# Gate bias seeded by ScalarE in PSUM for 15 of 36 blocks, three last adds on VectorE, and a new order, in a windowed-attention and highway kernel

## The chip, the cores and the metric

The kernel runs on one core of a Trainium2 chip. The metric is the device time of one execution in microseconds (us); a smaller number is better. Before the change the median of 3 runs is 156.6 us (155.8 to 159.38).

The engines are called PE or TensorE (matrix products, writing to PSUM), DVE or VectorE, ACT or ScalarE, POOL or GpSimd (which also issues all loads) and SP or SyncE (which issues the stores). PSUM has eight banks of 512 fp32 columns.

## The reference

Sliding-window attention with a linear distance bias, then a highway layer (cut to what matters):

```python
# q, k, v: (8, 8, 576, 64) float32: batch, heads, positions, head size
scores = q @ k^T / sqrt(64) - slope[head] * |i - j|      # only where 0 <= i - j < 128
attn = softmax(scores)
x = (attn @ v), heads side by side                       # (4608, 512)
H = relu(x @ w_h)
T = sigmoid(x @ w_t + b_t)                               # b_t: (512,), the gate bias
out = T * H + (1 - T) * x                                # (4608, 512) float32
```

## The kernel before

The attention is cut into 32 units (batch b of 8, group of four heads s of 2, half of the key tiles g of 2), and the highway layer into 36 blocks of 128 rows of x (four or five per batch; a block numbered 4 gathers the first 64 rows of two batches).

A unit takes these steps, each named by a letter. T (`tr`, L183): VectorE transposes loaded bf16 data of q or k. s (`scores`, L190): TensorE writes scores to banks 0 to 3. e (`soft`, L234): ScalarE takes the exponential to SBUF. m (`mask`, L241): VectorE multiplies with a table that holds the distance bias and the window; for the units in `MASK_PE` this step is left out, and four TensorE matmuls (L197) put the bias into PSUM ahead of the scores. p (`pv`, L246): TensorE multiplies with v and a column of ones, into two of banks 4 to 7. n (`norm`, L281): VectorE takes reciprocals and scales into x.

A block takes these. x and c (L311, L317): TensorE transposes x into PSUM and ScalarE copies it to SBUF. h (`mm_h`, L321): four matmuls with w_h. u (`relu_sub`, L333): VectorE computes relu(h) - x straight from PSUM (L339), or, for blocks in `RELU_ACT`, ScalarE first does the relu (r, L331) and VectorE subtracts from SBUF (L336). z (`mm_z`, L343): four matmuls with w_t, and a fifth (L349) that adds the bias as a product of `ones0`, whose first row is one, with `bT`, whose first row is the bias. a (`tanh`, L353): ScalarE takes the tanh of half the sum. t (L357, ScalarE) or, for blocks in `GATE_DVE`, k (L361, VectorE): the scaling 0.5 + 0.5 tanh, which gives T. g (`gate`, L366): VectorE multiplies T with relu(h) - x. o (`add_x`, L370): GpSimd adds x. d (`store`, L377): SyncE stores the rows.

L (`load`, L119) issues one of 60 loads from GpSimd's queue, in the order of the list `LOADS`; GpSimd runs loads and adds in one order. The loads cast fp32 in memory to bf16 in SBUF.

The work order is not left to a scheduler: the string `ORDER`, a plan made beforehand, is read letter by letter, and a digit behind s, p, x, h and z is the (first) PSUM bank. Each letter takes the next entry of its list, so each engine runs its instructions in the order in which they stand in the string. Banks 0 to 3 belong to the scores; p, x, h and z share banks 4 to 7. An instruction waits for whatever wrote its inputs and for whatever last used its outputs.

Of the kernel before, what the change touches and what calls it, by code (L numbers as in the profile page):

```python
# [9 lines left out]
P = 128  # L10
# [1 line left out]
NLD, NTR, NPB = 20, 12, 8  # L12


RELU_ACT = (1, 5, 6, 7, 8, 12, 14, 15, 16, 17, 23)
GATE_DVE = (0, 10, 16, 22, 24, 26, 28, 29)

LOADS = (0, 1, 3, 4, 2, 6, 5, 12, 16, 9, 14, 10, 13, 11, 17, 8, 15, 18, 20, 7, 21, 22, 27, 26, 19, 31, 29, 25, 30, 23, 24, 32, 33, 28, 34, 35, 39, 38, 40, 36, 41, 43, 37, 44, 46, 45, 53, 42, 47, 48, 58, 49, 52, 50, 56, 57, 51, 54, 59, 55)

MASK_PE = (6, 12)  # L20


ORDER = (
    "SLLSSLLLTLLTLs0LTLeLTLSms0LLp4LeLTLms0LLnp6eLLns0Lmx4ex5TLp6cms0cnep4Lz6nLmx7az4cTLSp6Tz"
    "5ns0ah6eh4ux7ks0mcrgap6Toth4enLdz5TLh6auLtux5Ls0ucx4eTx7z5gcTs0oah6cgLedmp4h7nous0rLdmh4"
    "tLez5Tp6grus0aonz4eTLdx5p6mcLs0th5nLaemp6z4ntgrx6Tx7aox5s0cgcducToh4ttp6mLdez5LnTp6rs0ag"
    "h4ueunoz5uLds0maLx4tp6Tez5gncos0az4TeLdx5mp6cLagLs0nth5eLTp6Lz4ontux6Lads0kmch5egh4mp6ru"
    "os0tnx4ez5Lduggh6mcx4z7gcToah4auodx5Trp6tods0cnh4eLdmz5LurgLx6maz7LtuLp4Tas0tLnh7coeTp4d"
    "h6gnros0rTx7p4cduex6z7nux4mz5acgcx7mz6atkTp4oats0nLdh6egp4Lguocs0Th6eLdnoz7uLx4dz5mcaLgh"
    "4amtx5p6Tocs0uh5edgz4noutp6amds0h4negh5uotx6Tz4cLdmp6as0rnz4egTox5p6aks0cLdnx4ez5umh6cTa"  # L30
    "h4ux5us0cz6geToh7mtds0akp4geuoh6nx7kdp4gcms0z7enouz4admp6amts0nx4h5cgp6uox4nz5cdgp6akotx"
    "4nh5egdz6uocx5h7cgdkgx4h5mcaz4uoup6oadtz5tdgz4ganoth5aodtx4h6ucgdx7z4uoch5gadotz4ugdh5ao"
    "tudgod"
)


def lists():

    units = [(b, s, g) for b in range(NB) for g in range(NG) for s in range(NS)]
    blocks = []  # L40
    for b in range(NB):
        blocks += [(b, 0), (b, 1)] + ([(b, 4)] if b % 2 else []) + [(b, 2), (b, 3)]
    trs = [(b, s, w) for b in range(NB) for s in range(NS) for w in range(2)]
    loads = []
    for b in range(NB):
        n = 1 if b < 2 else 2
        vs = [("v", b, n, m) for m in range(5)] if b < 2 or b % 2 == 0 else []
        ts = [("t", b, s, w) for s in range(NS) for w in range(2)]
        if b == 0:
            loads += ts[:2] + vs[:1] + ts[2:] + vs[1:3] + [("w", 0), ("w", 1), ("w", 2)] + vs[3:]  # L50
        else:
            loads += ts[:2] + vs[:3] + ts[2:] + vs[3:]
    by = dict(L=[loads[i] for i in LOADS], T=trs, S=list(range(5)))
    by.update({k: units for k in "sepn"})
    by["m"] = [u for i, u in enumerate(units) if i not in MASK_PE]
    by["pe_mask"] = [units[i] for i in MASK_PE]
    by.update({k: blocks for k in "xchuzagod"})
    by["r"] = [blocks[i] for i in RELU_ACT]
    by["k"] = [blocks[i] for i in GATE_DVE]
    by["t"] = [bk for i, bk in enumerate(blocks) if i not in GATE_DVE]  # L60
    return by
# [3 lines left out]
def kernel(  # L65
# [19 lines left out]
    ALU = mybir.AluOpType  # L85
# [4 lines left out]
    NC = DM // P  # L90
# [4 lines left out]
    by = lists()  # L95
# [23 lines left out]
    def load(kind, *at):  # L119
        if kind == "t":  # L120
            b, s, w = at
            nc.gpsimd.dma_start(
                out=LD[(4 * b + 2 * s + w) % NLD][:],
                in_=(q, k)[w][b, 4 * s : 4 * s + 4].rearrange("h (p t) d -> (h p) (t d)", t=NT))
        elif kind == "v":
            b, n, m = at
            rows, h = min(P, S - m * P), b % 2 * H
            nc.gpsimd.dma_start(  # L128
                out=VA[b // 2][0:rows, h : h + n * H, m, 0:D],
                in_=v[b : b + n, :, m * P : m * P + rows].rearrange("b h p d -> p (b h) d"))  # L130
        elif at[0] < 2:
            nc.gpsimd.dma_start(
                out=(wH, wT)[at[0]][:],
                in_=(moe_w_h, moe_w_t)[at[0]].rearrange("(c p) n -> p c n", p=P))
        else:
            nc.gpsimd.dma_start(out=bT[0:1, :], in_=moe_b_t.rearrange("(o n) -> o n", o=1))

    def setup(part):
        if part == 0:
            for i in range(NB // 2):  # L140
                nc.vector.memset(VA[i][:, :, :, D:E], 1.0)
            nc.vector.memset(PS[D:P, 0:4, 0:D], 0.0)
            nc.vector.memset(bT[:], 0.0)
            nc.vector.memset(ones0[:], 0.0)
            nc.vector.memset(ones0[0:1, :], 1.0)
            nc.vector.memset(ident[:], 1.0)
        elif part == 1:
            rel = cp.tile([P, 256], I32, name="rel_i")
            far = cp.tile([P, 256], F32, name="far")
            nc.gpsimd.iota(rel[:, 0:192], pattern=[[1, 192]], base=64, channel_multiplier=-1)  # L150
            nc.gpsimd.iota(rel[0:D, P:192], pattern=[[1, D]], base=0, channel_multiplier=-1)
            nc.gpsimd.iota(rel[:, 192:256], pattern=[[1, D]], base=0, channel_multiplier=-1)
            nc.gpsimd.affine_select(
                out=ident[:], in_=ident[:], compare_op=ALU.is_equal, fill=0.0,
                base=0, pattern=[[1, P]], channel_multiplier=-1)
            nc.vector.tensor_copy(out=REL[:], in_=rel[:])
            nc.vector.tensor_scalar(out=far[:], in0=REL[:], scalar1=-63.5, scalar2=None,
                                    op0=ALU.add)
            nc.vector.tensor_tensor(out=far[:], in0=far[:], in1=far[:], op=ALU.mult)
            nc.vector.tensor_scalar(out=far[:], in0=far[:], scalar1=4096.0, scalar2=1.0e6,  # L160
                                    op0=ALU.is_gt, op1=ALU.mult)
            nc.vector.tensor_tensor(out=REL[:], in0=REL[:], in1=far[:], op=ALU.add)
        elif part == 4:
            for h in range(H):
                nc.scalar.activation(out=SI[:, h, :], in_=ident[:], func=ACTF.Copy,
                                     scale=-slopes[h] / scale)
            nc.scalar.copy(out=RB[:, 0:D], in_=REL[:, 192:256])
# [175 lines left out]
    def mm_z(b, i, bank):  # L343
# [4 lines left out]
                             start=c == 0, stop=False)  # L348
        nc.tensor.matmul(out=pz, lhsT=ones0[:], rhs=bT[:], start=False, stop=True)  # L349

    def tanh(b, i):
        tt = TT[b, i] = ft.tile([P, DM], F16, name="tt")
        nc.scalar.activation(out=tt[:], in_=PZ.pop((b, i)), func=ACTF.Tanh, scale=0.5)  # L353
# [14 lines left out]
    def add_x(b, i):  # L368
        ot = OT[b, i] = ft.tile([P, DM], F32, name="ot")
        nc.gpsimd.tensor_tensor(out=like(ot[:], i), in0=like(UU.pop((b, i))[:], i),  # L370
                                in1=xview(b, i), op=ALU.add)

    def store(b, i):
        ot = OT.pop((b, i))
        if i < 4:
            row = b * S + D + i * P
            nc.sync.dma_start(out=out[row : row + P, :], in_=ot[:])  # L377
            return
        for r in range(2):
            row = (b - 1 + r) * S  # L380
            nc.sync.dma_start(out=out[row : row + D, :], in_=ot[r * D : (r + 1) * D, :])

    do = dict(L=load, T=tr, S=setup, s=scores, e=soft, m=mask, p=pv, n=norm, x=x_tr, c=x_copy,
              h=mm_h, u=relu_sub, z=mm_z, a=tanh, t=to_gate, k=to_gate_v, r=relu, g=gate, o=add_x, d=store)
    at = dict.fromkeys(by, 0)
    steps = iter("".join(ORDER))
    with tc.manual_schedule():
        for step in steps:
            what = by[step][at[step]]
            what = what if isinstance(what, tuple) else (what,)  # L390
            at[step] += 1
            if step in "spxhz":
                bank = int(next(steps))
                what += (bank,)
            do[step](*what)
# [30 lines left out]
```

## Time and profile before

| what | value |
|---|---|
| median of 3 runs | 156.6 us |
| the profiled execution | 156.49 us |
| its span, first to last instruction | 153.8 us |
| mean granted TensorE clock | 0.991 |
| L370 GpSimd add, 36 of them | 46.5 us, mean 1293 ns |
| L349 bias matmul on TensorE, 36 of them | 13.7 us, mean 379 ns |
| L353 tanh on ScalarE, 36 of them | 21.6 us, mean 601 ns |
| L357 gate scaling on ScalarE, 28 of them | 17.4 us, mean 629 ns |
| L361 gate scaling on VectorE, 8 of them | 3.4 us, mean 422 ns |
| L366 gate multiplication on VectorE, 36 of them | 17.9 us, mean 502 ns |
| L243 mask on VectorE, 15 of 1792 and 15 of 1536 columns | 17.2 us, mean 1145 ns; 14.4 us, mean 958 ns |

A line of the page's list of groups gives busy time, mean duration of one instruction, and the idle time of the engine ahead of it with what ended that. The rows of matmuls overlap: a 512-column matmul has a row of some 380 ns, while the next one starts 216 ns behind it. The stretches of the span (in us from its start) are cut where the chain of work that ended last changes its engine.

### The profile page before, as it was taken

To read this page: it belongs to the slowest core of one execution; us is meant where nothing else is said; L and a number is where in the kernel's file an instruction comes from. 1 tells how busy PE (TensorE), PEld (TensorE's weight loads), DVE (VectorE), ACT (ScalarE), POOL (GpSimd) and SP (SyncE) were. 2 spreads that over 40 slices of the span, in tenths; PEclk is the share of its full clock that TensorE was granted. 3 is DMA by queue.
4 is the path that set the end of the run, shared out by engine and by line. 5 is a ranking of instruction groups with operands and counts; after the bars stand their busy time and mean duration, and the time that the engine had idled before them with its cause. 6 is when DMAs were issued, how large, how long until landed. Compare 5 with 4: busy or idle time off the path is not lost.

```text
span 153.8 us, 5756 instructions
## 1 busy us (share of the span) xinstructions
PE 127.1 (83%) x2495; PEld 79.8 (52%) x2524; DVE 136.0 (88%) x220; ACT 115.4 (75%) x170; POOL 91.8 (60%) x104
## 2 busy tenths in 40 slices
PE   0027698999997998999959799799999999999950
PEld 0026584565655664665535566546575557644420
DVE  4865898699999999999999999999999999897650
ACT  3658476998998988898867969578887965667740
POOL 6986844157956467595889235797341370577562
PEclk9999999999999999999999999999999999999996
DMA  2999999999999989999999991899977212243353
GB/s 37 192 146 174 194 196 199 212 199 175 146 234 240 198 205 125 193 157 183 238 285 168 192 234 49 103 213 201 193 142 110 72 72 68 75 154 119 136 156 119
DMA packets 48233, 25.01 MB, mean 163 GB/s; under 512 B 38480, under 2 KB 39504, under 8 KB 48208
## 3 DMA queue, kind: packets, MB, share of 16 engines
q0 software_dynamic: 42960, 15.21, 91.8%
q1 hardware_dynamic: 5248, 9.44, 17.6%
q8 instruction: 19, 0.31, 0.8%
q14 instruction: 6, 0.05, 0.1%
HBM read 30.41 MB, written 9.44 MB: 259 GB/s over the span
## 4 chain that ended last, share of the span: by engine, by line
DVE 34%; PE 33%; DMA 15%; issue 9%; POOL 3%; ACT 1%; POOLq 1%; DVEq 0%; ACTq 0%
DVE tr L183 10%; PE ps L347 10%; PE ps L324 9%; DMA wT<-in_moe_w_t_dram 6%; DVE x L289 5%; DMA va<-in_v_dram 5%; DMA ld<-in_q_dram 5%; DVE p L243 5%; DVE uu L366 4%; DVE uu L339 3%; PE ps L212 3%; PE ps L275 3%; DVE uu L336 3%; PE ps L349 2%; PE ps L254 2%
## 5 line engine op out<-in xcount | busy, mean ns | idle before, releaser
L370 POOL TENSOR_TENSOR ot<-uu,x 128x512 f32<-128x512 bf16 x36 | 46.5, 1293 | 50.6 <-DVE uu L366 28.5
L238 ACT ACTIVATE p<-ps 128x1792 bf16<-128x1792 f32 (+1 forms) x32 | 49.9, 1559 | 12.3 <-PE ps L224 12.1
L183 DVE STREAM_TRANSPOSE tr<-ld 128x576 uint32<-128x576 uint32 x32 | 39.9, 1248 | 3.5 <-DMA ld<-in_q_dram 2.7
L347 PE MATMUL ps<-wT,xt 128*128 128x512 bf16 x132 | 36.3, 383 | 1.0 <-DMA wT<-in_moe_w_t_dram 0.3
L324 PE MATMUL ps<-wH,xt 128*128 128x512 bf16 x127 | 35.1, 381 | 1.1 <-issue 0.2
L243 DVE TENSOR_TENSOR p<-p,mt 128x1792 bf16<-128x1792 bf16 (+1 forms) x30 | 31.5, 1051 | 0.0
L353 ACT ACTIVATE tt<-ps 128x512 f16<-128x512 f32 x36 | 21.6, 601 | 8.7 <-PE ps L349 6.6
L212 PE MATMUL ps<-tr,tr 32*64 32x192 bf16 (+1 forms) x1024 | 18.2, 258 | 11.4 <-DVE tr L183 11.1
L128 POOL DMA_DIRECT2D va<-in_v_dram x25 | 25.4, 1019 | 1.8 <-DMA va<-in_v_dram 1.2
L319 ACT COPY xt<-ps 128x512 bf16<-128x512 bf16 x36 | 20.7, 587 | 6.4 <-PE ps L314 6.4
L289 DVE TENSOR_TENSOR x<-ps,rd 128x512 bf16<-128x512 f32 (+1 forms) x32 | 24.3, 758 | 1.2
L339 DVE SCALAR_TENSOR_TENSOR uu<-ps,x 128x512 bf16<-128x512 f32 x25 | 16.8, 682 | 3.9 <-PE ps L324 3.9
L212 PEld LDWEIGHTS <-tr 32*64 32x64 bf16 x1024 | 11.6, 111 | 16.4 <-DVE tr L183 11.6
L254 PE MATMUL ps<-va,p 128*128 128x65 bf16 x256 | 14.4, 200 | 6.8 <-DVE x L289 2.4
L347 PEld LDWEIGHTS <-xt 128*128 128x128 bf16 x144 | 12.7, 98 | 12.4 <-issue 0.8
L254 PEld LDWEIGHTS <-p 128*128 128x128 bf16 x256 | 12.1, 101 | 13.1 <-issue 7.4
L324 PEld LDWEIGHTS <-xt 128*128 128x128 bf16 x144 | 12.4, 98 | 12.3
L366 DVE TENSOR_TENSOR uu<-uu,tt 128x512 bf16<-128x512 bf16 x36 | 17.9, 502 | 0.8 <-ACT tt L357 0.3
L357 ACT ACTIVATE tt<-tt 128x512 f16<-128x512 f16 x28 | 17.4, 629 | 0.1
L275 PE MATMUL ps<-va,p 64*64 64x65 bf16 x448 | 14.9, 202 | 0.0
L314 PE MATMUL ps<-ident,x 128*128 128x128 bf16 x144 | 13.9, 224 | 0.7 <-DVE uu L339 0.7
L314 PEld LDWEIGHTS <-x 128*128 128x128 bf16 x144 | 10.2, 99 | 6.9 <-issue 1.6
(43 smaller groups left out, 107.3 us busy)
## 6 DMA issues: line engine op xcount, KB each, us to landing
out_dram<-ot SPq DMA_DIRECT2D x32, 256.0 KB, 3.8
ld<-in_q_dram POOLq DMA_DIRECT2D x16, 288.0 KB, 7.1
ld<-in_k_dram POOLq DMA_DIRECT2D x16, 288.0 KB, 8.0
va<-in_v_dram POOLq DMA_DIRECT2D x12, 256.0 KB, 7.4
va<-in_v_dram POOLq DMA_DIRECT2D x11, 128.0 KB, 6.8
out_dram<-ot SPq DMA_DIRECT2D x8, 128.0 KB, 2.4
wT<-in_moe_w_t_dram POOLq DMA_DIRECT2D x1, 512.0 KB, 8.5
wH<-in_moe_w_h_dram POOLq DMA_DIRECT2D x1, 512.0 KB, 10.8
```

The lines of the kernel that those rows point to most:

```text
L128: nc.gpsimd.dma_start(out=VA[b // 2][0:rows, h : h + n * H, m, 0:D], in_=v[b : b + n, :, m * P : m * P + rows].rearrange("b h p d -> p (b ...
L183: nc.vector.transpose(out=TR[i % NTR][:].rearrange("p s e -> p (s e)").bitcast(U32).rearrange("p (s t) -> p t s", t=NT), in_=LD[i % NLD][: ...
L212: nc.tensor.matmul(out=PS[r * D : r * D + D, bank + a, c0:c1], lhsT=KT[rows, lo + r * D : lo + r * D + D, e], rhs=QT[rows, q0 : q0 + c1 - ...
L238: nc.scalar.activation(out=PB[i][:, :, 0:w], in_=PS[:, bank : bank + 4, 0:w], func=ACTF.Exp, scale=scale)
L243: nc.vector.tensor_tensor(out=p[:, :, 0:w], in0=p[:, :, 0:w], in1=MT[s][:, :, 448 - w : 448] if g else MT[s][:], op=ALU.mult)
L254: nc.tensor.matmul(out=PS[:, bank + o, a * E : a * E + E], lhsT=p[:, a, col : col + P], rhs=VA[b // 2][:, b % 2 * H + 4 * s + a, i, :], st ...
L289: nc.vector.tensor_tensor(out=X[b, g][:, s, :, 0:n, :], in0=av[:, :, 0:n, 0:D], in1=rd[:, :, 0:n, :].to_broadcast([P, 2, n, D]), op=ALU.mult)
L314: nc.tensor.transpose(out=XP[b, i][:, c * P : (c + 1) * P], in_=xchunk(b, i, c), identity=ident[:])
L324: nc.tensor.matmul(out=pa, lhsT=XT[b, i][:, c, :], rhs=wH[:, c, :], start=c == 0, stop=c == NC - 1)
L347: nc.tensor.matmul(out=pz, lhsT=xt[:, c, :], rhs=wT[:, c, :], start=c == 0, stop=False)
L366: nc.vector.tensor_tensor(out=uu, in0=uu, in1=TT.pop((b, i))[:], op=ALU.mult)
L370: nc.gpsimd.tensor_tensor(out=like(ot[:], i), in0=like(UU.pop((b, i))[:], i), in1=xview(b, i), op=ALU.add)
```

## The change

For 15 blocks (`BIAS_ACT`) the step z is replaced by w and y. In w (`bias`), ScalarE copies the bias, now on all 128 partitions, into the block's PSUM bank; in y (`mm_y`), four matmuls that do not start a new sum add onto it. The fifth matmul falls away for these blocks. The bias is loaded into all 128 rows of `bT`, and the memset of `bT` is gone. The other 21 blocks keep z; there `ones0` still picks out the first row.

For the last three blocks (`ADD_DVE`), the add of x is done on VectorE (q) and not on GpSimd.

`MASK_PE` has four units in place of two, `GATE_DVE` 17 blocks in place of 8, `RELU_ACT` 12 in place of 11. `LOADS` and `ORDER` are new; they were planned with a rule that VectorE and GpSimd exclude each other in some instructions.

```diff
-RELU_ACT = (1, 5, 6, 7, 8, 12, 14, 15, 16, 17, 23)
-GATE_DVE = (0, 10, 16, 22, 24, 26, 28, 29)
+RELU_ACT = (2, 4, 7, 8, 12, 15, 16, 18, 21, 26, 30, 31)
+GATE_DVE = (0, 1, 2, 4, 5, 11, 14, 17, 21, 22, 24, 25, 26, 27, 28, 32, 33)
-LOADS = (0, 1, 3, 4, 2, 6, 5, 12, 16, 9, 14, 10, 13, 11, 17, 8, 15, 18, 20, 7, 21, ...)
+LOADS = (0, 1, 3, 4, 6, 5, 2, 12, 10, 13, 17, 11, 18, 8, 9, 7, 31, 15, 14, 16, 21, ...)
+BIAS_ACT = (1, 4, 8, 11, 12, 16, 18, 20, 23, 26, 27, 29, 32, 34, 35)
+ADD_DVE = (33, 34, 35)
-MASK_PE = (6, 12)
+MASK_PE = (7, 12, 14, 26)
...
-            nc.gpsimd.dma_start(out=bT[0:1, :], in_=moe_b_t.rearrange("(o n) -> o n", o=1))
+            nc.gpsimd.dma_start(
+                out=bT[:], in_=moe_b_t.rearrange("(o n) -> o n", o=1).to_broadcast([P, DM]))
...
-            nc.vector.memset(bT[:], 0.0)
...
+    def bias(b, i, bank):
+        PZ[b, i] = PS[:, bank, :]
+        nc.scalar.copy(out=PZ[b, i], in_=bT[:])
+
+    def mm_y(b, i):
+        for c in range(NC):
+            nc.tensor.matmul(out=PZ[b, i], lhsT=XT[b, i][:, c, :], rhs=wT[:, c, :], start=False,
+                             stop=c == NC - 1, skip_group_check=True)
...
+    def add_x_v(b, i):
+        ot = OT[b, i] = ft.tile([P, DM], F32, name="ot")
+        nc.vector.tensor_tensor(out=like(ot[:], i), in0=like(UU.pop((b, i))[:], i),
+                                in1=xview(b, i), op=ALU.add)
```

In `LOADS`, entry 8 is w_t, 9 the bias and 7 w_h; 0, 1, 3, 4 and 12, 13, 17, 18 are q and k of the first two batches, 2, 5, 6, 10, 11 the values of the first.

The end of the order, written here with the batch and block of each letter in place of the bank digits:

```
before: ... z74g70a71n711o63t71h71a74o70d63t74x72h74u71c72g71d70x73z72u74o71c73h72g74a72d71o74t72z73u72g72d74h73a73o72t73u73d72g73o73d73
after:  ... o63a71z74c72u71o70w72d63h74a74k71d70x73k74y72u74c73g71w73h72g74a72q74o71y73t72u72h73d71g72d74a73q72t73d72u73g73q73d73
```

More of the change, by code (lines that the diff above doesn't have):

```diff
@@ L12 @@
 NLD, NTR, NPB = 20, 12, 8
-RELU_ACT = (1, 5, 6, 7, 8, 12, 14, 15, 16, 17, 23)
-GATE_DVE = (0, 10, 16, 22, 24, 26, 28, 29)
-LOADS = (0, 1, 3, 4, 2, 6, 5, 12, 16, 9, 14, 10, 13, 11, 17, 8, 15, 18, 20, 7, 21, 22, 27, 26, 19, 31, 29, 25, 30, 23, 24, 32, 33, 28, 34, 35, 39, 38, 40, 36, 41, 43, 37, 44, 46, 45, 53, 42, 47, 48, 58, 49, 52, 50, 56, 57, 51, 54, 59, 55)
-MASK_PE = (6, 12)
-ORDER = (
[L24 to L33, printed above, removed]
@@ new lines @@
+RELU_ACT = (2, 4, 7, 8, 12, 15, 16, 18, 21, 26, 30, 31)
+GATE_DVE = (0, 1, 2, 4, 5, 11, 14, 17, 21, 22, 24, 25, 26, 27, 28, 32, 33)
+LOADS = (0, 1, 3, 4, 6, 5, 2, 12, 10, 13, 17, 11, 18, 8, 9, 7, 31, 15, 14, 16, 21, 27, 22, 20, 26, 23, 19, 30, 24, 25, 32, 33, 34, 29, 28, 39, 35, 38, 40, 48, 46, 43, 44, 45, 36, 37, 47, 42, 41, 51, 50, 53, 52, 49, 54, 56, 58, 57, 55, 59)
+BIAS_ACT = (1, 4, 8, 11, 12, 16, 18, 20, 23, 26, 27, 29, 32, 34, 35)
+ADD_DVE = (33, 34, 35)
+MASK_PE = (7, 12, 14, 26)
+ORDER = (
+    "SLLSSLLLTLLTLs0LTLeLLTSLms0LLp4eLTLms0nLp6eTLms0Lnp4eTLx6ms0cTx7eLz6nLcp4as0w6nLh7emh4Lk"
+    "ux5LyucSmp4h7ns0aTp4regx6nz7oTx4aLx5ds0cuLw7mLch6cTeLz4Tyaus0akgp4ekox6nh7LcdTp4rLs0uh6m"
+    "ez7gnots0uax4Lekz5dTLp6gaks0Tcox5h4cnLdez5mLh6tuamh7rtgs0grTow4p6eLudynLmx5as0cuop6eTx4h"
+    "5dgncos0tuLdp6eTLp4Lns0mx6z7cnez6ggap4Toas0w7nLdx6tyocTtp4dah6genox7uh4Lmdcx5Lw6s0gLh7cm"
+    "eyLukp4Taos0rnz6tLdegLTx7h4Lamh5ctus0oux6eh7uLdgz4Trocx5z7Tcdah5maw4p6mrs0tknyegp6guoz5n"
+    "atTLx4dp6acus0Lw5mh4enyoup6admts0h4enx5gp6Tocrs0nz5LedLgx4up6ckmLas0gw5h4noeyLgdx6uoh7cT"
+    "ax4z6LdtuocTh5aLdp6mrLs0nx4h5cgmep6z4uoutns0Ladmw5p6egx4nyocTx6h7dckaz4utgz5kagTop6as0on"
+    "dh4eTdx5p6cus0nw4h5emh6Tx7yrkcus0w6gx7agymcop4eodz7namp4das0nh6ekx7up4uckw6s0nh7kx4gygcg"
+    "oux4h5comdah4tuop6drex5nz4dkgh6cumaoz5rw4gdp6toayntdx5gx6uch7goaz5cuow4dh6akdx5kyucgw7h5"
+    "gaqoytuh4dgdaqtdugqd"
@@ L57, in lists @@
     by.update({k: blocks for k in "xchuzagod"})
+    by["w"] = by["y"] = [blocks[i] for i in BIAS_ACT]
+    by["z"] = [bk for i, bk in enumerate(blocks) if i not in BIAS_ACT]
+    by["q"] = [blocks[i] for i in ADD_DVE]
+    by["o"] = [bk for i, bk in enumerate(blocks) if i not in ADD_DVE]
     by["r"] = [blocks[i] for i in RELU_ACT]
@@ L383 @@
     do = dict(L=load, T=tr, S=setup, s=scores, e=soft, m=mask, p=pv, n=norm, x=x_tr, c=x_copy,
-              h=mm_h, u=relu_sub, z=mm_z, a=tanh, t=to_gate, k=to_gate_v, r=relu, g=gate, o=add_x, d=store)
+              h=mm_h, u=relu_sub, z=mm_z, a=tanh, t=to_gate, k=to_gate_v, r=relu, g=gate, o=add_x, d=store,
+              w=bias, y=mm_y, q=add_x_v)
     at = dict.fromkeys(by, 0)
@@ L391 @@
             at[step] += 1
-            if step in "spxhz":
+            if step in "spxhzw":
                 bank = int(next(steps))
```

## The prediction

> **What bounds the kernel now.** First the page: busy shares, then the slices, then the chain that ended last.
>
> ```profile
> PE 127.1 (83%) x2495; PEld 79.8 (52%) x2524; DVE 136.0 (88%) x220; ACT 115.4 (75%) x170; POOL 91.8 (60%) x104
> ...
> PE   0027698999997998999959799799999999999950
> ...
> DVE  4865898699999999999999999999999999897650
> ...
> DVE 34%; PE 33%; DMA 15%; issue 9%; POOL 3%; ACT 1%; POOLq 1%; DVEq 0%; ACTq 0%
> ```
>
> No engine stands out: VectorE and TensorE are both near full from about 30 us, and they share the chain. So I cut the span where the chain, in order of time, changes hands (VectorE's pieces fill it from 34 to 98 us, TensorE's from 98 to 148) and asked for busy time by stretch.
>
> ```profile
> 35.00:98.00 63.00, 56.77 (x1203) 35.66 (x1217) 61.95 (x95) 54.50 (x75) 41.26 (x43) 1.00 1.39 185
> 98.00:148.00 50.00, 48.58 (x821) 29.07 (x831) 46.25 (x80) 36.87 (x53) 27.11 (x24) 1.00 0.67 130
> 148.00:153.80 5.80, 0.20 (x1) 0.00 (x0) 1.12 (x2) 0.63 (x1) 2.01 (x2) 0.75 0.44 137
> ```
>
> Columns: PE, weight load, DVE, ACT, POOL. In the first stretch VectorE is busy 61.95 of 63 us (98%), TensorE 90%; in the second TensorE 97%, VectorE 92%. Relief of one engine helps only until the other binds: TensorE has some 6 us of slack in the first stretch.
>
> VectorE's busy time is not all work. Its timeline and GpSimd's around 75 us:
>
> ```profile
> 75.17 2.04 DVE L243 TENSOR_TENSOR p<-p,mt 128x1792 bf16<-128x1792 bf16 x1
> 77.13 1.37 DVE L366 TENSOR_TENSOR uu<-uu,tt 128x512 bf16<-128x512 bf16 x1
> ...
> 75.06 3.16 POOL L370 TENSOR_TENSOR ot<-uu,x 128x512 f32<-128x512 bf16 x2 [0.73 <-DVE uu L366]
> ```
>
> Undisturbed, this mask takes 1.08 us and this gate 0.415. Each began just after a GpSimd add had begun and finished 0.96 us late; the second add in turn ran long (2.00 against 1.15 us). PSUM-reading subtractions, norms and transposes beside such adds keep their time; masks, gates, gate scalings and SBUF subtractions do not. Over the run 12 instructions are held for 7.3 us, 7 of them for 5.1 us in the first stretch.
>
> The start and the end:
>
> ```profile
> 14.94 8.54 DMA wT<-in_moe_w_t_dram
> 23.53 0.61 PE ps L347
> ...
> 149.10 0.42 DVE L366 TENSOR_TENSOR uu<-uu,tt 128x512 bf16<-128x512 bf16 x1
> 149.66 1.15 POOL L370 TENSOR_TENSOR ot<-uu,x 128x512 f32<-128x512 bf16 x1 [0.79 <-POOL ot L370]
> ```
>
> TensorE reaches its first gate matmul and waits for the weights; at the end the last add is GpSimd's, followed by a store.
>
> **The change, part by part,** against the profiled execution: 156.49 us, of which 153.8 are the span and 2.7 lie around it (the median of the runs is 156.6).
>
> *Start.* The gate weights are the 14th load in GpSimd's queue, not the 16th, and wH the 16th, not the 20th; value loads go back. The wait above cost 0.26 us ahead of the first matmul and some 0.6 us between it and the second (23.53 to 24.36, where neighbours stand 0.215 apart): 0.9 us. Two loads fewer ahead (0.56 and 0.95 us to issue) cover it. The memset of the bias tile that goes (0.27 us) ran while VectorE still waited for its first load. The bias, now 128 rows and behind the weights instead of ahead, is wanted only after the four weight matmuls (0.86 us). Ends: 0 (attention work of that moment is no earlier) and -1.5. I take **-0.9**.
>
> *First stretch, VectorE's own work.* Gate scalings there go from 2 to 7: 5 x 0.282 = +1.4 us. Two blocks return from ScalarE's relu to the subtraction from PSUM: 2 x (0.68 - 0.41) = +0.5. One mask goes to TensorE (unit 14; unit 7 replaces 6, an equal swap): -0.95. Net **+1.0**. TensorE loses 6 bias matmuls here (6 x 0.216; another of the 15 ran at 26 us) and gains a mask (0.65); VectorE paces this stretch, so I count neither.
>
> *The holds.* The new order was planned with this exclusion. The 5.1 us can go entirely. They can also grow: instructions that can be held go from 85 (36 gates, 30 masks, 11 SBUF subtractions, 8 scalings) to 96, 13% of 5.1 = +0.7. Read off the two orders, the instructions standing within 1.2 us behind a gate, where its add would run, include 34 that can be held before (36 adds) and 36 after (33 adds). That shows no cure, but ignores how long an add waits behind loads. Nothing favours an end: I take the middle, **-2.2**, and keep +0.7 and -5.1.
>
> *Second stretch, TensorE.* Eight of the 15 bias matmuls ran after 98 us: 8 x 0.216 = -1.7; a mask (unit 26) adds 4 x 0.163 = +0.65 (row mean 326 ns less the 163 ns by which a matmul's row outlasts its spacing). **-1.1.** VectorE, close behind, loses that mask (-0.95); 4 more scalings (+1.1) and 4 fewer PSUM subtractions (-1.1) cancel. Ends: 0 (VectorE or the seeds bind) and -1.7.
>
> *Seeds.* Copying bf16 from SBUF to fp32 in PSUM is not in the trace; 512-wide ScalarE rows lie between 0.587 and 0.629 us. 15 x 0.59 = +8.9, nine scalings fewer 9 x 0.63 = -5.7, a relu +0.6: ScalarE +3.8 to 119 us. I cost it at nothing: TensorE reaches the add-on one to four steps after the seed was queued, and ScalarE idles 38 us in all. The cover is thin from 40 to 55 us, where ScalarE is busy 14.04 of 15 us. Behind each seed stand exponentials and x copies that TensorE needs. If the cover is gone everywhere: +8.9; the other end is 0.
>
> *Tail.* For the last three blocks the add follows the gate on VectorE. The gate ends at 149.52, GpSimd's add at 150.81. An fp32-writing add 512 wide lies between the gate's 0.415 and the PSUM subtraction's 0.68 us; fp32 tensor ops of 256 columns take 0.425, so I take 0.69, of which 0.08 overlaps the gate: 150.13, **-0.7**. The stores on SyncE wait for VectorE instead of GpSimd. Ends: -0.9, and 0 if the two earlier adds (1.3 us) push the last gate; they lie beside TensorE's last two groups (1.7 us).
>
> Sum: -0.9 + 1.0 - 2.2 - 1.1 - 0.7 = -3.9; 156.5 - 3.9 = **152.6 us**.
>
> **Rivals.**
>
> *Seeds in the way (slower).* Seven of the 15 seeds go to a bank last read by a relu step, six of those on VectorE, which is 98% busy in the first stretch; ScalarE, in order, waits there with an exponential behind it, and TensorE waits for both. For: the thin stretch. Against: TensorE has other steps between. If each seed holds TensorE for its 0.59 us: 152.6 + 8.9 = 161.5. It decides from 0.47 us per seed (7.1 us over 15), 159.7.
>
> *Holds stay.* The chip's order of starts differs from the planned one, so adds still catch masks. For: the count of 34 and 36. No gain at the start, and +1.0 + 0.7 - 1.1 - 0.7: 156.4, no change.
>
> *Holds vanish.* -0.9 + 1.0 - 5.1 - 1.1 - 0.7 = -6.8: 149.7. Against: TensorE would have to run the first stretch at 97%.
>
> *Loads starved.* Gate scalings on VectorE might hold up GpSimd's load issue, not only its adds. In this trace no scaling overlaps a load's issue, so no row decides it. Nine more at 0.28 us, all on the path: +2.5, 155.1. The Trainium skill says this (SBUF — State Buffer, section "SBUF: two separate sides"): a VectorE instruction that uses both port pairs locks GpSimd out, descriptor writing for its DMAs included. What the trace shows agrees as far as adds go (the 0.96 us above); for loads, by the page, the sum would be 155.1 instead of 152.6.
>
> **How the numbers follow.** Forecast 0.40 (own range 150.7 to 154.5: the holds half-way to either end are 1.45 us, start and tail 0.45), holds stay 0.25, seeds in the way 0.19, holds vanish 0.13, loads starved 0.03. About 2% is what a measurement of this kernel can tell from no change: 153.5 and 159.7. Faster: 0.31 of the forecast and 0.13 = 0.44. Same: 0.09 + 0.25 + 0.03 = 0.37. Slower: 0.19. From 149.0 to 158.0 the range takes in all but the seeds' case.
>
> **What would show it.** Right: the mean of the gates (L366 before, 502 ns) falls toward 415 and fewer VectorE rows run 0.96 us long; the seeds' rows take about 0.59 us and hardly any matmul waits for them; the first gate matmul starts before 23 us; the last VectorE add ends under 0.7 us after its gate. Wrong: TensorE or ScalarE's exponentials waiting on seeds, ScalarE waiting on VectorE's subtractions, as many long rows as before, or TensorE under 90% after 98 us.

## The result, and the profile after

The changed kernel takes 161.19 us (median of four runs, 160.24 to 161.3) against 156.45 for the kernel before on the same chip: a ratio of 1.0304, 95% interval 1.0245 to 1.0363. It is 4.7 us slower where 3.9 us faster was forecast. Medians here and below are over all executions of a kernel; ratios leave out those over 1.5% longer than its fastest. The profiled execution took 161.23 us, with a span of 159.5 (before: 156.49 and 153.8).

The page of the changed kernel: busy time of each engine, and the chain that ended last, by engine.

```profile
PE 126.9 (80%) x2488; PEld 79.7 (50%) x2517; DVE 143.6 (90%) x229; ACT 119.7 (75%) x177; POOL 87.6 (55%) x101
...
DVE 49%; PE 18%; DMA 15%; issue 10%; POOL 3%; ACT 2%; DVEq 0%; POOLq 0%
```

VectorE is 7.6 us busier than before, and its share of the chain rose from 34 to 49%; TensorE's fell from 33 to 18%. The same stretches as before (columns: PE, weight load, DVE, ACT, POOL, granted clock) say where:

```profile
35.00:98.00 63.00, 57.34 (x1237) 35.88 (x1250) 60.97 (x97) 54.65 (x74) 39.63 (x42) 1.00 1.39 179
98.00:148.00 50.00, 44.00 (x785) 26.71 (x781) 48.29 (x78) 37.60 (x54) 25.83 (x24) 1.00 0.63 124
148.00:159.50 11.50, 5.34 (x28) 2.37 (x26) 8.25 (x14) 4.72 (x9) 2.46 (x3) 0.91 0.40 138
```

Up to 98 us TensorE is level with before (57.34 us busy against 56.77). Between 98 and 148 us it falls from 48.58 to 44.00 us, 88% where before it had 97%, while VectorE rises to 97%. The work that TensorE lost there is done after 148 us (5.34 us against 0.20).

VectorE is full but does less, because it is held behind GpSimd far more often. Undisturbed durations are as before (mask 1.08 or 0.95 us, gate 0.415, SBUF subtraction 0.415, scaling 0.282); the new add on VectorE takes 0.69. What each row has above them, added up over the rows that are over by 60 ns or more:

| stretch | before | after |
|---|---|---|
| to 98 us | 7 held, 5.1 us | 5 held, 3.8 us |
| 98 to 148 us | 5 held, 2.2 us | 11 held, 8.3 us |
| from 148 us | none | 2 held, 1.5 us |
| sum | 12 held, 7.3 us | 18 held, 13.7 us |

The sum grew by 6.4 us, the span by 5.7. All 12 rows before are held behind adds. Of the 18 after, 16 are, for 12.1 us; the other two are scalings held for 1.6 us behind GpSimd's issue of value loads (last section). Which instruction is held can be read in two places. First the changed kernel at 128 us, then the kernel before at 124 us, each from its timeline (start and duration in us; x2 is two instructions in a row):

```profile
127.42 0.74 DVE L382 TENSOR_TENSOR uu<-uu,tt 128x512 bf16<-128x512 bf16 x2
...
127.96 3.17 POOL L386 TENSOR_TENSOR ot<-uu,x 128x512 f32<-128x512 bf16 x2 [6.35 <-DVE uu L382]
...
128.07 2.05 DVE L250 TENSOR_TENSOR p<-p,mt 128x1792 bf16<-128x1792 bf16 x1
```

```profile
124.16 0.42 DVE L366 TENSOR_TENSOR uu<-uu,tt 128x512 bf16<-128x512 bf16 x1
...
124.50 1.09 DVE L243 TENSOR_TENSOR p<-p,mt 128x1792 bf16<-128x1792 bf16 x1
...
124.71 1.88 POOL L370 TENSOR_TENSOR ot<-uu,x 128x512 f32<-128x512 bf16 x1 [0.82 <-DVE uu L366]
```

In the second place the mask stands directly behind a gate. It starts 0.21 us before that gate's add, keeps its 1.09 us, and the add takes 1.88 us instead of 1.15. In the first place there are two gates and then the mask: the first gate's add starts while the second gate runs, 0.11 us before the mask, and the mask takes 2.05 us. So whichever starts first keeps its time, and the other waits it out. An add starts 0.13 us behind the end of its gate, and the next VectorE instruction, if it waits for nothing, some 0.08 us before that end: the first instruction behind a gate wins and the second can lose. In both traces no instruction of these kinds that began 0.16 to 0.23 us ahead of an add (11 before, 12 after) is more than 12 ns over its time. The changed order has more places where a gate with an add on GpSimd is followed by one instruction under 0.5 us and then by one that can be held: 8, before 3.

The other steps of the prediction in the trace: the chain of the start, the seeds, and the end of VectorE's timeline.

```profile
5.54 7.23 DMA va<-in_v_dram
12.77 0.28 issue
13.05 10.47 DMA wT<-in_moe_w_t_dram
...
23.57 0.58 PE ps L354
24.15 0.22 issue
24.37 1.06 PE ps L354 x2
```

```profile
L360 ACT CAST ps<-bT x15: 589/597/632, 26.5 to 150.4; 128x512 f32<-128x512 bf16 x15
...
  DVE uu L346: 1.6, 2
who waited for it (us, times):
```

```profile
155.41 0.43 DVE L382 TENSOR_TENSOR uu<-uu,tt 128x512 bf16<-128x512 bf16 x1
155.87 0.69 DVE L391 TENSOR_TENSOR ot<-uu,x 128x512 f32<-128x512 bf16 x1
```

The weights' load was issued 1.89 us earlier and took 10.47 us instead of 8.54, so the first gate matmul starts where it did (23.57, before 23.53). The seeds take 597 ns at the median, and no wait is put down to them: the list in the last line is empty. ScalarE itself waited 1.6 us, twice, to write them. The last add on VectorE ends 0.72 us behind its gate, where GpSimd's ended 1.29 behind it.

### The profile page after: what moved, and what is told of

Its sections match the earlier page's. It is cut to its first block, busy times and chain, and to the rows that moved or that the text cites. A ratio compares the mean times of both kernels' runs of the same rounds, so it can differ in the third digit from the quotient of the medians.

```text
span 159.5 us, 5747 instructions
## 1 busy us (share of the span) xinstructions
PE 126.9 (80%) x2488; PEld 79.7 (50%) x2517; DVE 143.6 (90%) x229; ACT 119.7 (75%) x177; POOL 87.6 (55%) x101
## 4 chain that ended last, share of the span: by engine, by line
DVE 49%; PE 18%; DMA 15%; issue 10%; POOL 3%; ACT 2%; DVEq 0%; POOLq 0%
DVE tr L190 10%; DVE p L250 10%; DMA va<-in_v_dram 8%; DVE uu L382 7%; DVE x L296 7%; DMA wT<-in_moe_w_t_dram 7%; DVE uu L346 6%; PE ps L331 6%; DVE uu L343 4%; DVE tt L377 2%; PE ps L354 2%; DVE rd L295 2%; PE ps L282 2%; PE ps L219 2%; PE ps L261 2%
## 5 line engine op out<-in xcount | busy, mean ns | idle before, releaser
L386 POOL TENSOR_TENSOR ot<-uu,x 128x512 f32<-128x512 bf16 x33 | 42.3, 1286 | 53.2 <-DVE uu L382 28.3
L245 ACT ACTIVATE p<-ps 128x1792 bf16<-128x1792 f32 (+1 forms) x32 | 49.9, 1559 | 11.2 <-PE ps L231 10.9
L219 PE MATMUL ps<-tr,tr 32*64 32x192 bf16 (+1 forms) x1024 | 18.7, 262 | 12.2 <-DVE tr L190 11.3
L219 PEld LDWEIGHTS <-tr 32*64 32x64 bf16 x1024 | 11.9, 112 | 17.1 <-DVE tr L190 12.3
L331 PEld LDWEIGHTS <-xt 128*128 128x128 bf16 x144 | 12.6, 98 | 12.8 <-issue 1.0
L382 DVE TENSOR_TENSOR uu<-uu,tt 128x512 bf16<-128x512 bf16 x36 | 17.1, 492 | 0.4
L321 PE MATMUL ps<-ident,x 128*128 128x128 bf16 x144 | 14.5, 225 | 3.2 <-DVE x L296 3.1
L346 DVE SCALAR_TENSOR_TENSOR uu<-ps,x 128x512 bf16<-128x512 f32 x24 | 16.2, 680 | 0.1
L373 ACT ACTIVATE tt<-tt 128x512 f16<-128x512 f16 x19 | 12.1, 635 | 0.2
```

The costliest lines, as they stand in the source:

```text
L219: nc.tensor.matmul(out=PS[r * D : r * D + D, bank + a, c0:c1], lhsT=KT[rows, lo + r * D : lo + r * D + D, e], rhs=QT[rows, q0 : q0 + c1 - ...
L245: nc.scalar.activation(out=PB[i][:, :, 0:w], in_=PS[:, bank : bank + 4, 0:w], func=ACTF.Exp, scale=scale)
L321: nc.tensor.transpose(out=XP[b, i][:, c * P : (c + 1) * P], in_=xchunk(b, i, c), identity=ident[:])
L331: nc.tensor.matmul(out=pa, lhsT=XT[b, i][:, c, :], rhs=wH[:, c, :], start=c == 0, stop=c == NC - 1)
L346: nc.vector.scalar_tensor_tensor(out=like(uu[:], i), in0=like(PA.pop((b, i)), i), scalar=0.0, in1=xview(b, i), op0=ALU.max, op1=ALU.subtract)
L382: nc.vector.tensor_tensor(out=uu, in0=uu, in1=TT.pop((b, i))[:], op=ALU.mult)
```

## The experiments

Theory A: the 4.7 us are VectorE being held behind GpSimd's adds. Rivals: the seeds (B), the gate scalings moved to VectorE (C), the new list of loads (D). Each ratio is to the kernel before, measured beside it. The holds are those of the one profiled execution. Where a kernel says "before" or "after" it starts from that one.

| kernel | us, median | ratio, 95% interval | VectorE held |
|---|---|---|---|
| after | 161.19 | 1.030 (1.025 to 1.036) | 18, 13.7 us |
| before, add without its reads | 151.16 | 0.965 (0.954 to 0.975) | 3, 0.9 us |
| after, add without its reads | 153.35 | 0.979 (0.969 to 0.988) | 3, 1.7 us |
| after, no seeds | 161.05 | 1.030 (1.023 to 1.037) | 20, 14.0 us |
| after, 12 scalings on ScalarE | 160.57 | 1.027 (1.019 to 1.036) | 16, 12.3 us |
| after, add in two halves | 156.83 | 1.008 (1.003 to 1.013) | 23, 9.6 us |
| before, add in two halves | 152.96 | 0.981 (0.974 to 0.988) | 12, 4.4 us |
| after, old list of loads | 167.18 | 1.072 (1.065 to 1.079) | 17, 13.0 us |
| after, no reads, old list | 160.46 | 1.028 (1.019 to 1.036) | 3, 1.1 us |
| after, no reads, list by first use | 151.20 | 0.964 (0.956 to 0.972) | 5, 1.6 us |
| after, halves, list by first use | 157.32 | 1.005 (0.999 to 1.010) | 24, 10.7 us |
| before, halves, last three adds on VectorE | 152.31 | 0.976 (0.965 to 0.986) | 13, 4.8 us |
| before, add in quarters | 155.99 | 0.986 (0.973 to 0.999) | 27, 5.2 us |
| before with seeds, wide bias load, last adds | 160.63 | 1.030 (1.021 to 1.038) | 12, 7.1 us |
| the same, halves | 157.85 | 1.011 (1.002 to 1.020) | 14, 5.1 us |
| after, no relu on ScalarE | 159.94 | 1.025 (1.015 to 1.035) | 15, 8.1 us |
| after, list by first use | 160.31 | 1.029 (1.019 to 1.039) | 20, 13.8 us |
| before with seeds, halves, narrow bias load | 154.31 | 0.989 (0.985 to 0.993) | 14, 5.0 us |
| after, narrow bias load | 160.85 | 1.032 (1.028 to 1.035) | 19, 13.8 us |

### Adds that read one column

The same edit in both kernels: GpSimd adds one column and writes the rest with two memsets, about as long as the add. It also ends the adds' own waits for VectorE (before, they take 5.1 us more than 1.15 us each, after 4.4), which no run separates from VectorE's.

```diff
-        nc.gpsimd.tensor_tensor(out=like(ot[:], i), in0=like(UU.pop((b, i))[:], i),
-                                in1=xview(b, i), op=ALU.add)
+        nc.gpsimd.tensor_tensor(out=ot[:, 0:1], in0=UU.pop((b, i))[:, 0:1],
+                                in1=xview(b, i)[:, 0, 0:1], op=ALU.add)
+        nc.gpsimd.memset(ot[:, 1:DM], 0.0)
+        nc.gpsimd.memset(ot[:, 1:DM], 0.0)
```

> The kernel before, in its order, but GpSimd's add is replaced: it adds one column only (so that it still waits for the gate) and then writes zeros over the other 511 columns twice; the output thus leaves out the last add. GpSimd keeps its place in the order but hardly reads SBUF. Theory A (the holds of VectorE behind GpSimd's adds set the difference): the 12 holds of 7.3 us fall under 2 us, and the time falls from 156.5 to 150.5-153.5, since some 4.5 us of the holds lay on the chain. Theory B (seeds and the new order set the difference) says nothing of this run but needs it as a base. Theory C (the extra VectorE work sets it) likewise.

> The changed kernel with the same replacement of GpSimd's adds (the three adds on VectorE stay). Theory A: its 18 holds of 13.7 us fall under 2.5 us and the time falls from 161.2 to 150-153.5, to within 1 us of the kernel before with the same replacement or below it. Theory B: it stays at least 3.5 us above that one, near 157. Theory C: it stays some 2 us above it.

Measured: 151.16 and 153.35 us. Against 156.45 and 161.19 the kernel before gained 5.3 us and the changed one 7.8; the difference between them fell from 4.7 to 2.2 us (their intervals overlap). The 2.2 us are also what rival C expected here. The chain of the kernel before, so edited, is TensorE's (it was 34% DVE, 33% PE); that of the changed kernel, so edited, is led by transfers:

```profile
PE 48%; DVE 20%; DMA 15%; issue 7%; POOL 4%; ACT 3%; POOLq 0%; DVEq 0%; ACTq 0%
```

```profile
DMA 30%; DVE 28%; PE 22%; POOL 11%; issue 6%; ACT 0%; DVEq 0%; POOLq 0%
```

Of the waits of TensorE in that kernel, this line is for values: 2.8 us in four waits, the longest 1.2.

```profile
PE ps L261 <- DMA va<-in_v_dram: 2.8, 4, 1.2
```

So A carries about half of the difference outright, and a second cause lies under it. The line points to the loads; the runs with other lists, below, test that.

### Without seeds, and with the old scalings

In the first kernel the 15 blocks get their five matmuls back, at the place of y; in the second, 12 of the 17 scalings return to ScalarE, at the place of k.

```diff
-        nc.scalar.copy(out=PZ[b, i], in_=bT[:])
+        PZ[b, i] = bank
...
+        mm_z(b, i, PZ[b, i])
```

> The changed kernel without the seeds: ScalarE copies nothing into PSUM, and the 15 blocks take the four matmuls and the bias matmul again at the place of the add-on. Theory B: the time falls by 4 us or more, to 157 or less. Theory A: it stays within 1.5 us of 161.2; TensorE has 15 x 0.216 = 3.2 us more work, ScalarE 8.9 us less, and neither sets the end.

> The changed kernel with 12 of its 17 gate scalings on ScalarE at the same places in the order (all but those that the kernel before has on VectorE too). VectorE loses 12 x 0.28 = 3.4 us of work and three holds of 2.2 us; ScalarE gets 7.5 us. Theory C (extra VectorE work): 161.2 falls to 157-158. Theory A: it falls by the holds that go, about 2 us, and by part of the work, to 157.5-160, and the time follows the total of the holds in the trace. Theory B: no gain or a loss (161-165), since ScalarE is what is late.

Measured: 161.05 and 160.57 us. Fifteen seeds fewer (ScalarE 112.7 us busy instead of 119.7) and 15 matmuls more changed nothing: B falls. Twelve scalings fewer on VectorE (3.4 us at 0.282) gave 0.6 us, which lies inside the intervals. That fits none of the three theories' ranges, A's neither: 3.4 us of work and 1.3 us of holds less on VectorE should by A have given more. ScalarE got the scalings (125.0 us busy instead of 119.7), so this run does not clear C by itself; the sorted list below does.

### Halved adds

Each add is cut into two of 256 columns (0.66 to 0.68 us undisturbed), so that a held instruction waits for half as long.

```diff
-        nc.gpsimd.tensor_tensor(out=like(ot[:], i), in0=like(UU.pop((b, i))[:], i),
-                                in1=xview(b, i), op=ALU.add)
+        uu, xv = like(UU.pop((b, i))[:], i), xview(b, i)
+        m = 2 if i == 4 else 1
+        for j in range(2):
+            part = slice(j * m, j * m + m)
+            nc.gpsimd.tensor_tensor(out=like(ot[:], i)[:, part], in0=uu[:, part],
+                                    in1=xv[:, part], op=ALU.add)
```

> The changed kernel with each of GpSimd's adds cut into two adds of 256 columns. Theory A (the holds behind GpSimd's adds): a VectorE instruction can then start between the halves, so a hold is 0.5 us at most instead of 0.96, the total of the holds falls from 13.7 to 6-8 us, and the time falls from 161.2 to 155-158. If holds are not what costs (the new order itself, late values): GpSimd has 33 more instructions of some 0.15 us, and the time stays at 160-162.

> The kernel before with each add cut into two of 256 columns. Theory A: the holds fall from 7.3 to 3-4.5 us, and the time from 156.5 to 153-155. Otherwise 156-158.

Measured: 156.83 and 152.96 us. The holds fell by 4.0 and 2.8 us, the ratios by 0.022 and 0.019, some 3.5 and 2.9 us: about one for one, with the whole computation in place. That is A's mechanism, near its price. The changed kernel kept more holds than the 6 to 8 us expected, because it has more of them (23, with whole adds 18). Elsewhere a microsecond of holds was worth less: with one-column adds 6.4 us fewer gave 5.3 us before, and 12.0 fewer gave 7.8 after. Most of the difference between the two kernels stays (3.9 us), as do 5.2 us of holds between them (9.6 against 4.4).

### The loads

The changed kernel with the old `LOADS`, as it is and with the adds that read one column; then with a list sorted by the place in the order at which each load is first used, with one-column adds, with halved adds and with whole adds.

```diff
-LOADS = (0, 1, 3, 4, 6, 5, 2, 12, 10, 13, 17, 11, 18, 8, 9, 7, 31, 15, 14, 16, 21, 27, 22, 20, ...)
+LOADS = (0, 1, 3, 4, 6, 5, 2, 12, 13, 10, 11, 17, 18, 8, 9, 7, 15, 14, 16, 21, 22, 26, 27, 20, ...)
```

> The changed kernel, its letters as they are, but each load letter takes the next load of the list of the kernel before (values of the second batch earlier, weights and q, k later). Theory D (values that land late make up what the holds leave): 161.2 falls by 1-2.5 us, to 158.7-160.2. Theory A alone: within 1 us of 161.2, unless the holds happen to fall elsewhere, which their total in the trace would show.

> The same list of loads in the changed kernel whose GpSimd adds hardly read SBUF (one column added, zeros written twice over the rest; the last add is left out of the output). Theory D: 153.4 falls by 1.5-2.5 us to the 151 of the kernel before with the same replacement, since TensorE no longer waits 2.8 us for values. If the rest of the difference lies in the order of the other steps: it stays within 0.8 us of 153.4.

> The changed kernel whose GpSimd adds hardly read SBUF (one column added, zeros over the rest; the last add is left out of the output), its letters as they are, with the list of loads sorted by the place of first use in the order: k of batch 3, 6 and 5 and values of batches 4 and 6, issued 20 to 35 us ahead of use, go back, and the values of the first two odd batches come forward. Theory D (loads issued too early make the urgent ones late): TensorE's waits for values, 2.8 us, mostly go, and 153.4 falls by 1-2.5 us to 151-152.4, near the 151.2 of the kernel before with the same replacement. If the remaining difference lies in the steps themselves: 153-154.

> The changed kernel with halved adds and the list of loads sorted by first use. Theory D on top of theory A: from 156.8 to 154.5-156. Without D: 156-157.5.

> The changed kernel, full adds, with the list of loads sorted by first use. If late loads cost beside the holds (theory D): 158.5-160. If VectorE, held, sets the pace and covers the late loads: 160.5-162.

Measured: 167.18, 160.46, 151.20, 157.32 and 160.31 us. The old list was a miss in both kernels: VectorE's transposes wait for k and q, as this line of its waits shows for the first of them, because the old list is not made for the new order.

```profile
DVE tr L190 <- DMA ld<-in_k_dram: 7.9, 4, 3.3
```

The sorted list settles D for the kernel without holds: 151.20 us, 2.2 less than with the new list (the four executions of each do not overlap), and level with the kernel before under the same edit (0.964 against 0.965). This kernel has all 15 seeds and 17 scalings, so without holds neither B nor C costs anything either. TensorE's wait for values shrank from 2.8 us to this:

```profile
PE ps L261 <- DMA va<-in_v_dram: 0.5, 1, 0.5
```

With the holds in place the sorted list gives 0.9 us by the medians (160.31), inside the intervals, and with halved adds nothing. So the loads' lateness shows only where the holds are gone; the likely reason, not tested by itself, is that values are needed later as long as VectorE is late.

### The features in the old order

The order and the lists of before, with 13 seeds put up to eight steps ahead of their matmuls, the bias load into 128 rows at its old, tenth place, and the last three adds on VectorE; then the same with halved adds. Beside them the kernel before with halved adds and the last three adds on VectorE, and one with quartered adds.

```diff
-        nc.gpsimd.tensor_tensor(out=like(ot[:], i), in0=like(UU.pop((b, i))[:], i),
+        if (b, i) in ((7, 4), (7, 2), (7, 3)):
+            nc.vector.tensor_tensor(out=like(ot[:], i), in0=like(UU.pop((b, i))[:], i),
+                                    in1=xview(b, i), op=ALU.add)
+            return
...
```

> The kernel before with halved adds, and its last three adds on VectorE at their places in the order. The tail term of the prediction (-0.7 us): 153.0 falls to 152.0-152.7. If VectorE's three adds of 0.69 us push its last steps instead: 153-154.

> The kernel before with each add cut into four of 128 columns. Theory A: a hold is at most some 0.3 us, the total falls from 4.4 (halves) to 2-3 us, and the time from 153.0 to 151.5-152.7. Against it: an add of 256 columns takes 0.66 us and one of 512 1.15, so four of 128 take some 1.65 us, 0.5 more per block; if GpSimd's longer adds delay loads and the last store, 153-155.

> The kernel before with its order, lists and loads, into which two parts of the change are put: 13 seeds by ScalarE (where the bank was last written by a full-width matmul group; each as early as its bank is free, at most eight steps ahead of the add-on), the bias loaded on all partitions, and the last three adds on VectorE. Theory A (the new order makes VectorE be held more often; the parts themselves do no harm): 154.5-157, holds 6-9 us. If the parts themselves are at fault: 159 or more.

> The same with each GpSimd add cut into two of 256 columns. Theory A: holds near 4.5 us and 151.5-153.5, against 152.3 for the same without seeds. If seeds hold up TensorE once the holds are short: 154 or more.

Measured: 152.31, 155.99, 160.63 and 157.85 us. The first has the lowest median of all that compute everything, 2.4% under the kernel before; from the halves alone (152.96) it can't be told apart. Quarters were a miss: 2 to 3 us of holds were expected and 5.2 measured, and 144 adds keep GpSimd busy for 110.9 us. Whether they take longer than halves is not shown: the intervals overlap, and in the profiled executions (156.19 and 152.98 us) 1.7 us of the difference is there at 32 us, before the first add.

The two with seeds end 3.6 and 4.4 us above their expected ranges, though they hold VectorE about as long as the kernels they come from (7.1 us against 7.3, 5.1 against 4.8). Against the 152.31 us kernel VectorE's transposes in the halved one are 1.2 us late at 25 us and 4.1 at 32 us. Its first seed stands at 36.5 us, so the seeds did not make these 4.1 us. From there to 101 us the lag stays, and to the end it grows by 1.9. On GpSimd's timeline ahead of that point a load waits for the bias:

```profile
14.56 0.74 POOL L139 DMA_DIRECT2D wT<-in_moe_w_t_dram  x1 [0.62 <-DMA ld<-in_q_dram]
15.55 0.88 POOL L135 DMA_DIRECT2D va<-in_v_dram  x1 [0.26 <-DMA va<-in_v_dram]
17.51 0.55 POOL L129 DMA_DIRECT2D ld<-in_k_dram  x1 [1.08 <-DMA bT<-in_moe_b_t_dram]
```

### The bias load by itself

The load goes into one row again, and the memset of the tile is back, in the kernel of 157.85 us and in the changed kernel.

```diff
-            nc.gpsimd.dma_start(
-                out=bT[:], in_=moe_b_t.rearrange("(o n) -> o n", o=1).to_broadcast([P, DM]))
+            nc.gpsimd.dma_start(out=bT[0:1, :], in_=moe_b_t.rearrange("(o n) -> o n", o=1))
...
+            nc.vector.memset(bT[:], 0.0)
```

> The kernel before with halved adds, 13 seeds and the last three adds on VectorE (157.85 us before this edit), and now with the bias loaded into one row again, the other 127 rows of the tile zero: seeded blocks then lack the bias in 127 of their rows, which leaves out part of the computation. If the load of 128 rows makes the loads behind it late: the 4.0 us lost between 24 and 34 us come back, 153.9 us, and the weights' load lands before 24 us. If the seeds themselves, or the steps moved for them, are what costs: 157.5 to 158 us.

> The changed kernel with the bias loaded into one row and the memset of the tile back; seeded blocks lack the bias in 127 of their rows, so part of the computation is left out. Here the load stands behind that of the gate weights. Theory (VectorE held behind GpSimd's adds makes most of the 4.7 us): 160 to 161.2 us, 17 to 20 held instructions, at most 1.2 us faster. Rival (the load of 128 rows is a cause of its own weight here too): 157 to 159 us, and the norms of the first units 2 to 4 us earlier.

Measured: 154.31 and 160.85 us. Ahead of the weights, the wide load costs 3.5 us by the medians (the intervals, 0.985 to 0.993 and 1.002 to 1.020, lie apart), and 1.9 us between the two profiled executions (157.85 and 155.94 us). There the first gate matmul starts at 23.8 us instead of 24.9. Behind the weights, where the change put it, the load costs nothing that can be told from noise. The two kernels with the old list, above, had the wide load at that place as well, so their misses mix two causes.

In the old order 2.0 us stay between 154.31 and 152.31. The traces show where the profiled executions (155.94 and 151.81 us) part: 2.1 us by 32 us, none from there to 101 us, 2.0 us behind that. The first 2.1 us come ahead of the first seed (34.5 us). They are TensorE's: four gate matmuls, in the 152.31 us kernel and then in the one with the narrow bias load:

```profile
24.67 1.03 PE L347 MATMUL ps<-wT,xt 128*128 128x512 bf16 x4
```

```profile
23.80 1.89 PE L354 MATMUL ps<-wT,xt 128*128 128x512 bf16 x4 [0.58 <-DMA wT<-in_moe_w_t_dram]
```

The second kernel's rows last 0.63 us and start 0.43 us apart until 27 us, where the first kernel's last 0.38 and start 0.216 apart. With the wide load this goes on to 30 us. The column of the granted clock gives 1.00 for these stretches in all three. What sets the moment of the change is not shown. Behind 101 us the seeds may count: over the run ScalarE waits 5.5 us to write them into banks that VectorE still reads, and TensorE 1.8 us for them. No run separates that.

### Without relu on ScalarE

All subtractions are made from PSUM, so that 12 instructions that can be held are gone; in some blocks the bank holds a later sum by the time the subtraction reads it, so their values differ.

```diff
-        rr = RR[b, i] = fx.tile([P, DM], BF16, name="rr")
-        nc.scalar.activation(out=rr[:], in_=PA.pop((b, i)), func=ACTF.Relu)
+        return
```

> The changed kernel without ScalarE's relu: its 12 blocks are subtracted straight from PSUM, which GpSimd's adds do not hold. VectorE gets 12 x 0.27 = 3.2 us of work, and the five held subtractions (4.4 us) can't be held any more. Theory A: the holds fall from 13.7 to 9-11 us and the time to 159.5-161 (holds less work). If VectorE's own work set the pace and not the holds: 162-164.5.

Measured: 159.94 us. The holds fell by 5.5 us, the time by 1.3 (the intervals overlap): each of the 12 now takes 0.68 us where it took 0.41 undisturbed (3.2 us more). A hold that is bought off with a longer instruction is no gain of its whole length.

## Why the prediction was wrong, point by point

*The holds* are the step that failed: -2.2 us predicted (ends +0.7 and -5.1), +6.4 us of held time measured. The upper end was "13% of 5.1", as if holds grew with the number of instructions that can be held. They do not: taking 12 scalings away lowered them by 1.3 us of 13.7. With whole adds the six kernels in the new order that keep their relu steps hold 12.3 to 14.0 us, with or without the seeds, the scalings, the new list or the wide bias load; the two in the old order hold 7.1 and 7.3. The gates' mean, which was to fall from 502 toward 415 ns, is 492. The evidence at hand, 34 against 36 instructions within 1.2 us behind a gate, was not counted by one rule: the rule that gives 34 for the old order gives 39 for the new one. And it was counted in the wrong window: it put the first instruction behind a gate, which wins, beside the second, which loses. Also, the step looked at the first stretch alone, where the holds did fall (5.1 to 3.8 us); they grew by 6.1 us in the second, which was costed as TensorE's, and by 1.5 in the tail.

A better count could have been made from the two orders. Set VectorE's instructions behind each gate in a row at their undisturbed durations, each 0.08 us ahead of its predecessor's end and waiting for nothing else; start the add 0.13 us behind the gate for 1.15 us; let an instruction that begins earlier keep its time, and hold the first that begins later until the add ends. This estimate gives 8.3 us for the order of before and 10.9 for the new one. If an add that meets a running instruction waits for that one first, as in the second place above, it gives 11.8 and 14.6. Either way the new order holds VectorE 2.6 to 2.8 us longer: the sign is right, but it is little more than half of the 4.8 us by which the holds behind adds grew. It was worked out after the result, and no run changed only the places of these instructions. That the new order, with its lists, makes the holds is shown by the eight kernels; that it does so by the second places is argued, and in part open. That the holds cost time is shown by the one-column and the halved adds.

*Second stretch, TensorE*, -1.1: failed with the holds. The prediction named the sign for it, TensorE under 90% after 98 us, and it is 88%. Its bound "VectorE binds" was set at 0, as if VectorE could not get worse there.

*Start*, -0.9: not there. The load, two places further ahead, was issued 1.89 us earlier and was 1.93 us longer on its way, so the earlier issue bought nothing. Behind the first gate matmul the next rows last 0.63 us (before 0.50 and 0.38), and the bias matmul that ends the group starts at 25.23 us instead of 24.91. The places came from two value loads of the second batch and the bias, which went back; a q or k load of that batch went ahead. TensorE waits 1.4 us for values, before 0.9.

*First stretch, VectorE's own work*, +1.0: not separable. VectorE's busy time without holds is 57.1 us there, before 56.9, but by 98 us not quite the same work is done.

*Seeds*, 0: right. 597 ns where 0.59 us was taken, and leaving them out changed nothing. The rival "seeds in the way" gave 161.5 us and the result is 161.2; the kernel without seeds (161.05) shows that the agreement is chance. A time that fits is no evidence for a mechanism.

*Tail*, -0.7: 0.57 us at the last block, as the two rows above show; the add started 0.03 us behind its gate instead of ahead of its end. But another of the three adds on VectorE was itself held by GpSimd, 1.53 us instead of 0.69. In the old order the step gave 0.65 us (152.96 to 152.31), less than its interval.

*Loads starved*, the rival with 0.03, named loads held by scalings. The prediction said that no scaling overlaps a load's issue in the trace of before, so that no row decides it. Two do: those at 94.81 and 114.87 us run into value-load issues that begin at 95.84 and 115.11 us, and these issues take 1.20 and 0.86 us, as others do. The reverse, scalings held by issues, is below. What the loads did cost is another thing, a list that sends for some values before others that are needed sooner: 2.2 us, and visible only where the holds are gone.

With one-column adds, and the sorted list in the changed one, the two kernels take the same time (151.20 and 151.16). So the sum of the prediction's other terms, -1.7 us, was not there either; whether a better order would have collected it stays open.

## What to carry to other kernels

Where two engines exclude each other, look at who starts first: the instruction directly behind the one that releases the other engine wins, the next one can pay in full, so count the second places and not the neighbourhood. Replay an order with that rule before trusting that it was planned for it, and shorten the instruction that holds (two halves gave 2%, four gave no more). Remove the leading cause in both kernels before judging the next: the loads' 2.2 us could not be seen under the holds. And before a loss is put down to a step, look where in the span it arises: the 4.1 us of the kernel with seeds were lost before its first seed.

## What the runs showed of the hardware

The exclusion has two conditions. An add that reads its 512 columns holds masks, gates and SBUF subtractions whole; memsets that write as many columns hold none of them. Scalings are held by memsets as well: one that began 0.22 us behind the start of such a memset took 0.45 us instead of 0.28. The Trainium skill ("SBUF — State Buffer", section "SBUF: two separate sides") says that the pair of ports is an exclusive lock which goes to whoever starts first, and that instructions with two SBUF inputs meet it only against a GpSimd instruction that reads SBUF. Both traces and the one-column adds agree, with the 0.96 us and the 12 ns above.

Scalings wait for GpSimd's issue of value loads too. The changed kernel's timeline at 99.7 us:

```profile
98.76 2.32 POOL L135 DMA_DIRECT2D va<-in_v_dram  x2
...
99.71 1.48 DVE L377 TENSOR_SCALAR tt<-tt 128x512 f16<-128x512 f16 x1
...
101.07 1.19 POOL L386 TENSOR_TENSOR ot<-uu,x 128x512 f32<-128x512 bf16 x1
101.11 1.97 DVE L250 TENSOR_TENSOR p<-p,mt 128x1536 bf16<-128x1536 bf16 x1
```

The scaling takes 1.48 instead of 0.28 us and ends 0.11 us behind the two issues; gate and subtraction beside the same issues keep their time (0.41 and 0.42), as do two scalings beside the issue of q (282 and 288 ns). In the kernels with the sorted list three scalings that began 0.03 to 0.18 us behind the start of a value issue kept theirs too (282 and 283 ns). The mask behind the held scaling is then held by the add, so one place costs 2.2 us.

A load of one 512-element row into 128 partitions, ahead of the weights, took 8.5 us to land where the load into one partition took 7.1, and the weights behind it took 10.3 us instead of 8.9; the whole took 3.5 us more by the medians.

TensorE starts slowly in every profile here: eight matmuls of 128x65 take 0.62 us at first and 0.41 later, and rows of 512 columns, where they come early enough, 0.63 and 0.38. The change comes between 20 and 30 us, while the column of the granted clock gives 1.00 throughout. Only two profiles, the kernel before with one-column adds and the changed one with these and the old list, have an entry there: a granted clock of 0.50 for 3.4 us, from 24 and from 32 us, with slow rows. Two pairs of profiles whose steps are the same up to 32 us, halves and quarters of the kernel before and the two shown above under the bias load, differ by 1.7 and 2.1 us at that point, with the later change in the slower one.
